# Block sums of weights loaded behind the unit loads, operand sums formed a product sooner, eight PSUM banks in turn

## The chip, the cores and the metric

The kernel runs on one core of a Trainium2 chip. The metric is the device time of one execution in microseconds; several executions are timed and their median is given. The profile is of one such execution. Engines are named as the profile names them: PE (TensorE matmul) and PEld (its weight load), DVE (VectorE), ACT (ScalarE), POOL (GpSimd) and SP, whose queue issues nearly all DMAs.

## The reference

Attention with normalized queries and keys, a feed-forward layer with a squared ReLU, and a gated layer with two more products:

```python
# q, k, v: (4, 12, 448, 64); x: (1792, 768)
q_n, k_n = rmsnorm(q, g_q), rmsnorm(k, g_k)
attn = softmax(q_n @ k_n^T / sqrt(64))
x = rows(attn @ v)                       # (1792, 768)
h = x @ w_in                             # (768, 2048)
x = maximum(h, 0)**2 @ w_out             # (2048, 768)
out = ((x @ w1) * (x @ w2)) @ w3 @ w_out2   # (768, 1024) twice, (1024, 1024), (1024, 768)
```

The weights arrive as 64-bit floats, the rest as 32-bit floats.

## The kernel before

The program walks over 48 attention heads (4 batches of 12) and fills the gaps of each head's chain with matmuls of other work. Beside the heads of batch 0 stands the product of `w3` with the last weight, kept in DRAM as `w3o`; beside those of batch 1 the feed-forward part of batch 0; beside those of batches 2 and 3 first the feed-forward part of batch 1 and then the first product (`w_in`) of batch 2, in `gen_in(PB)`, late in the heads of batch 3. When the heads end, near 945 us, there follows the **tail**, `gen_pair`: `gen_in(PB + 1)`, which is `w_in` for batch 3, and then the products with `w_out` (called L2 here), with `w1` and `w2` (L3) and with `w3o` (L4) for batches 2 and 3 together. L2, L3 and L4 are done as block products by a scheme with seven products instead of eight for a 2 by 2 block matrix. `ORDER2` and `ORDER3` name the seven; `a11`, `a12`, `a21`, `a22` are the operand's blocks, `sums_of` makes the operand sums that products 6, 7 and 4 need, and product 3 needs `a12` less a sum.

Every multiplication is of numbers in two halves: `hi` is the number rounded by an ACT copy to the matmul's type (L112), `lo` the rest, subtracted on POOL or DVE (L120), and three matmuls (L362, L363, L364, in `mm3`) make one product. L120 and L112 are helpers, so the profile's lines for them mix many uses; the tile names tell them apart: `hl` is a weight unit's two halves, `op` an operand's, `quad` the blocks of a weight sum.

Weights come in **units** of 128 by 384 or 128 by 512. `advance` loads a unit into `raw` (L280, six buffers), splits it into `hl` and keeps a few units ahead of the matmul that uses it. Products 5, 4, 7 and 6 need sums of weight blocks. There are 17 of these **sums** (`quads`): six for L2, eight for L3, three for L4. `fetch_next` loads two tiles of 128 by 2 by 512 (or 384) into `quad` (L244), of which four buffers exist, `sum_next` does four subtractions on them and stores two tiles `qs` to DRAM (L260), and the unit loads read them from there. `sum_step` does one `sum_next` for what has been fetched and one `fetch_next`. In `gen_in` it is called for every second product, on POOL (`"g"`) for batch 2 and on DVE (`"v"`) for batch 3.

Instructions of one engine run in the order in which the scheduler of the language put them at build time; it orders by priority and by its own idea of when inputs are there, and a buffer that is free early lets a load move far ahead of the code around it. SP's queue too is in order: a DMA whose wait is not met holds all behind it. The order of the work below is therefore told by the built program, not by the source alone.

In the heads of batches 1 to 3 the softmax result `p` is sent through a DMA to `pw` (L882), and PE transposes `pw` (L903) for the product with `v`.

In L2 a product has eight operand steps `i`, each with three output tiles of three matmuls (nine matmuls), and `form` makes the operand halves `op` some steps ahead by `form2`. `gather` adds a finished product from its PSUM bank to the running sums on DVE (L512). `bank` gives L2's output banks; L3 and L4 take theirs from `ps_mm`, which has three. `after2` turns L2's results into L3's operands.

## Time and profile before

| what | value |
|---|---|
| median of the runs (lowest, highest) | 1292.01 us (1289.71, 1300.1) |
| the profiled execution's own time | 1294.27 us |
| its span in the profile | 1292.5 us |
| PE busy | 1173.5 us (91%), 6078 matmuls |
| PEld, DVE, ACT, POOL busy | 1046.5, 922.3, 737.0, 809.5 us |
| mean granted clock of TensorE | 0.951 |
| 16 DMA engines, mean over the span | 182 GB/s |

The span is what the profiler saw of the program's instructions; 1.8 us of the execution lie outside it. A granted clock of 1.00 is TensorE's upper level of 2.4 GHz and 0.5 its lower of 1.2 GHz; a stretch between the two has some of both. PE at 91% is not PE at its full pace: a matmul at the lower level counts as busy for longer.

### The profile page before, as it was taken

To read this page: it belongs to the slowest core of one execution; us is meant where nothing else is said; L and a number is where in the kernel's file an instruction comes from. 1 tells how busy PE (TensorE), PEld (TensorE's weight loads), DVE (VectorE), ACT (ScalarE), POOL (GpSimd) and SP (SyncE) were. 2 spreads that over 40 slices of the span, in tenths; PEclk is the share of its full clock that TensorE was granted. 3 is DMA by queue.
4 is the path that set the end of the run, shared out by engine and by line. 5 is a ranking of instruction groups with operands and counts; after the bars stand their busy time and mean duration, and the time that the engine had idled before them with its cause. 6 is when DMAs were issued, how large, how long until landed. Compare 5 with 4: busy or idle time off the path is not lost.

```text
span 1292.5 us, 19021 instructions
## 1 busy us (share of the span) xinstructions
PE 1173.5 (91%) x6078; PEld 1046.5 (81%) x6078; DVE 922.3 (71%) x1461; ACT 737.0 (57%) x1595; POOL 809.5 (63%) x772
## 2 busy tenths in 40 slices
PE   7799999988989896589989999999999979899998
PEld 4688888877878786578778888898999969789888
DVE  5798889779978872587889777766432586764574
ACT  5799876667556643455555566656644436433442
POOL 5875536656766677754466565544465779765675
PEclk9799999999989898799999999999999979899999
DMA  7775558888788778677775455554334323233332
GB/s 219 234 239 164 179 176 253 266 292 259 255 237 247 248 248 282 208 230 237 251 256 191 136 151 149 158 162 139 113 102 125 98 65 107 64 109 109 114 125 81
DMA packets 125093, 235.17 MB, mean 182 GB/s; under 512 B 13024, under 2 KB 74688, under 8 KB 124992
## 3 DMA queue, kind: packets, MB, share of 16 engines
q1 hardware_dynamic: 121536, 228.44, 57.2%
q10 hardware_dynamic: 3456, 5.51, 1.2%
q8 instruction: 48, 0.79, 0.3%
q14 instruction: 53, 0.43, 0.1%
HBM read 161.74 MB, written 43.25 MB: 159 GB/s over the span
## 4 chain that ended last, share of the span: by engine, by line
PE 37%; DVE 11%; DMA 6%; POOL 4%; issue 3%; ACT 2%; SPq 0%; POOLq 0%; DVEq 0%; ACTq 0%
PE mm L362 10%; PE mm L363 10%; PE mm L364 10%; DMA pw<-p 2%; DMA quad<-f 2%; PE pt L903 2%; POOL hl L120 1%; ACT p L876 1%; DVE quad L120 1%; POOL quad L120 1%; DVE op L120 1%; PE kv L955 1%; DVE g L120 1%; DVE nb L859 1%; DMA kn<-k_nat 1%
## 5 line engine op out<-in xcount | busy, mean ns | idle before, releaser
L120 POOL TENSOR_TENSOR hl<-raw,hl 128x384 fp32r<-128x384 f32 (+1 forms) x366 | 436.8, 1201 | 221.1 <-ACT hl L112 213.3
L112 ACT ACTIVATE hl<-raw 128x384 fp32r<-128x384 f32 (+1 forms) x399 | 221.3, 563 | 148.2 <-PE mm L364 86.1
L363 PE MATMUL mm<-x,hl 128*128 128x448 f32 (+1 forms) x640 | 239.6, 374 | 9.4 <-POOL x L120 9.4
L362 PE MATMUL mm<-x,hl 128*128 128x448 f32 (+1 forms) x640 | 244.1, 381 | 4.2 <-DVE xf L969 2.0
L364 PE MATMUL mm<-x,hl 128*128 128x448 f32 (+1 forms) x640 | 237.8, 372 | 0.0
L876 ACT ACTIVATE p<-sc,nb,rr 112x448 f32<-112x448 f32 x192 | 137.3, 720 | 121.4 <-DVE nb L860 121.1
L362 PE MATMUL mm<-op,hl 128*128 128x448 f32 x348 | 131.2, 379 | 12.2 <-ACT op L112 8.1
L363 PEld LDWEIGHTS mm<-x,hl 128*128 128x128 f32 x640 | 124.8, 195 | 20.3 <-POOL x L120 11.1
L363 PE MATMUL mm<-act,hl 128*128 128x448 f32 (+1 forms) x352 | 132.7, 377 | 6.8 <-POOL act L120 6.6
L363 PE MATMUL mm<-op,hl 128*128 128x448 f32 x348 | 131.8, 379 | 6.0 <-POOL op L120 5.0
L362 PEld LDWEIGHTS mm<-x,hl 128*128 128x128 f32 x640 | 124.3, 194 | 15.4 <-issue 2.3
L362 PE MATMUL mm<-act,hl 128*128 128x448 f32 (+1 forms) x352 | 134.8, 383 | 0.0
L120 DVE TENSOR_TENSOR ptr<-pt,ptr 128x448 fp32r<-128x448 f32 x144 | 86.5, 617 | 65.3 <-ACT ptr L112 64.8
L364 PEld LDWEIGHTS mm<-x,hl 128*128 128x128 f32 x640 | 124.6, 195 | 10.2 <-POOL hl L120 0.5
L364 PE MATMUL mm<-op,hl 128*128 128x448 f32 x348 | 130.9, 376 | 0.0
L364 PE MATMUL mm<-act,hl 128*128 128x448 f32 (+1 forms) x352 | 130.7, 372 | 0.0
L297 POOL TENSOR_SCALAR raw<-raw 128x384 uint32<-128x384 uint16 (+1 forms) x110 | 80.6, 733 | 74.8 <-DMA raw<-w_in 19.0
L859 DVE TENSOR_REDUCE nb<-sc 112x1 f32<-112x448 f32 x192 | 113.8, 615 | 14.1 <-PE sc L858 12.7
L304 DVE SCALAR_TENSOR_TENSOR raw<-raw 128x384 uint32<-128x384 uint32 (+1 forms) x120 | 88.9, 746 | 37.6 <-POOL hl L120 24.4
L291 ACT ACTIVATE raw<-raw 128x384 f32<-128x384 f32 (+1 forms) x120 | 70.0, 596 | 59.0 <-DMA raw<-w 19.5
L857 PE MATMUL sc<-kt,qh 128*112 128x448 f32 x192 | 76.7, 400 | 26.1 <-ACT p L876 25.1
L903 PE MATMUL pt<-ident_r,pw 112*128 112x112 f32 (+1 forms) x576 | 62.9, 247 | 37.6 <-DMA pw<-p 32.1
(147 smaller groups left out, 2429.3 us busy)
## 6 DMA issues: line engine op xcount, KB each, us to landing
pw<-p SPq DMA_DIRECT2D x72, 392.0 KB, 4.0
raw<-f_in SPq DMA_DIRECT2D x96, 192.0 KB, 2.4
raw<-w_in SPq DMA_DIRECT2D x32, 384.0 KB, 4.9
raw<-w_out SPq DMA_DIRECT2D x24, 512.0 KB, 5.6
raw<-w SPq DMA_DIRECT2D x32, 384.0 KB, 4.2
qt<-q_t SPq DMA_DIRECT2D x48, 224.0 KB, 3.4
raw<-f_out SPq DMA_DIRECT2D x42, 256.0 KB, 2.8
raw<-f SPq DMA_DIRECT2D x56, 192.0 KB, 2.4
```

The lines of the kernel that those rows point to most:

```text
L112: nc.scalar.activation(out=out, in_=in_, func=AF.Copy)
L120: e.tensor_tensor(out=out, in0=in0, in1=in1, op=ALU.subtract)
L291: nc.scalar.activation(out=hi, in_=hi, func=AF.Prelu, scale=2.0**-112, alpha=-(2.0**32))
L297: nc.gpsimd.tensor_scalar(out=t[:, :n, 0], in0=low, scalar1=2.0**-13, scalar2=2.0**-14 - 0.5, op0=ALU.mult, op1=ALU.add)
L304: nc.vector.scalar_tensor_tensor(out=f[:, :n].bitcast(U32), in0=t[:, :n, 1], scalar=3, in1=t[:, :n, 0], op0=ALU.logical_shift_left, op1=AL ...
L362: nc.tensor.matmul(ps, w[:, 0, wk, :], x[0], start=(i == 0), stop=False)
L363: nc.tensor.matmul(ps, w[:, 0, wk, :], x[1], start=False, stop=False)
L364: nc.tensor.matmul(ps, w[:, 1, wk, :], x[0], start=False, stop=(i == last))
L857: nc.tensor.matmul(o[j], d["qh"][:, c * P:(c + 1) * P], d["kt"], start=True, stop=False)
L859: nc.vector.tensor_reduce(out=nb[:, j:j + 1], in_=o[j], axis=AX.X, op=ALU.max, negate=True)
L876: nc.scalar.activation(out=p, in_=o[j], func=AF.Exp, scale=d["rq"][:, c:c + 1], bias=nb[:, j:j + 1], accum_out=sm[:, i, c:c + 1],)
L903: nc.tensor.transpose(to[:kn, c * P:(c + 1) * P], d["p"][c][:, k0:k0 + kn], one)
```

## The change

Five edits. (1) In `fetch_next` each load of a `quad` may not stand ahead of the last unit load that the source has issued (`issue_after`). (2) `gen_in` calls `sum_step` three times for each batch (products 2, 7 and 12) instead of eight, the loop that finished all sums ahead of L2 goes, and `sum_step("v")` is called behind each of L2's seven products and after each group of seven in L3. (3) `sums_of` and the subtraction for product 3 run one product sooner, behind product 2's and product 6's operands; the spare tiles of L2 take other buffers for that. (4) `form` runs four steps ahead in L2 instead of three. (5) The output tiles of L2, L3 and L4 go round eight banks of four pools.

```diff
     def fetch_next():
...
-            nc.sync.dma_start(out=t, in_=src)
+            with tc.issue_after(last["load"]):
+                nc.sync.dma_start(out=t, in_=src)
...
     def load_next():
...
-            nc.sync.dma_start(out=t[:, :n], in_=src)
+            last["load"] = nc.sync.dma_start(out=t[:, :n], in_=src).ins
...
     def gen_in(b):
...
-            if m % 2:
+            if m % 5 == 2:
                 sum_step("g" if b == PB else "v")
...
-    def bank(k):
-        if k % 2 == 0:
-            return ps_mm.tile([128, 512], F32, name="mm", tag="mm")[:, :S]
+    banks = [(ps_mm, "mm"), (ps_sc, "sc"), (ps_mm, "mm"), (ps_pt, "pt")]
+    banks += [(ps_mm, "mm"), (ps_sc, "sc"), (ps_kv, "kv"), (ps_pt, "pt")]
+
+    def bank():
+        pool, tag = banks[turn["ps"] % len(banks)]
         turn["ps"] += 1
-        pool, tag = ((ps_sc, "sc"), (ps_sc, "sc"), (ps_pt, "pt"))[turn["ps"] % 3]
         return pool.tile([128, 512], F32, name=tag, tag=tag)[:, :S]
...
     def gen_pair():
         yield from gen_in(PB + 1)
-        while pos["sum"] < len(quads):
-            sum_step("v")
...
         def form2(k, i):
+            src = {1: a[i][0], 2: a[i][1], 6: a[i][0], 7: spare.get(i), 4: a[i][3], 5: a[i][2], 3: a[i][1]}[k]
+            t = parts(src, xp, "x", "v" if i % 2 else "g")
+            if k == 2:
+                if i < 4:
+                    spare[i] = t2.tile([128, S], F32, name="s3", tag=("khl", "vhl")[i // 2])
+                elif i % 2 == 0:
+                    x = xp.tile([128, 2, S], F32, name="s3", tag="x")
+                    spare[i], spare[i + 1] = x[:, 0, :], x[:, 1, :]
+                sums_of(a[i], spare[i])
             if k == 6:
...
-                sums_of(a[i], spare[i])
-            if k == 3:
                 sub_on("v", a[i][1], a[i][1], a[i][0])
...
-            ps = [bank(m) for _ in range(NQ)]
+            ps = [bank() for _ in range(NQ)]
...
-                    form(m * n + at + 3, form2)
+                    form(m * n + at + 4, form2)
...
             after2(k)
+            sum_step("v")
```

In L3 `ps` comes from `bank()` and `sum_step("v")` stands behind each group of seven products; in L4 `ps` comes from `bank()` too and `form4` moves its sums as `form2` does.

What moves where, from the built programs. The number behind a name counts buffers; before and after count differently from L2 on.

**SP's queue, in the heads of batch 2.** `f_in` and `f_out` units are of the feed-forward part of batch 1. Before:

```order
L260 DMA qs3_0_116<-quad_10255 128x1024
L260 DMA qs3_1_117<-quad_10257 128x1024
L280 DMA raw_5905<-f_in_106 128x384
L260 DMA qs4_0_118<-quad_10373 128x1024
L746 DMA qt_5889<-q_t 128x448
L882 DMA pw_5829<-p_5826 112x896
L280 DMA raw_5938<-f_in_106 128x384
```

After:

```order
L282 DMA raw_5905<-f_in_106 128x384
L752 DMA qt_5889<-q_t 128x448
L282 DMA raw_5938<-f_in_106 128x384
L888 DMA pw_5829<-p_5826 112x896
L282 DMA raw_5957<-f_in_106 128x384
```

Loads and stores of the sums are gone from here. In the changed program the first load of a `quad` stands in `gen_in(PB)`, behind a unit of `f_in` for batch 2.

**SP's queue and DVE, where L2's product 4 ends and product 5 runs.** `f_out_107` and `f_1_108` are units of products 3 and L3's first; `qs10` and `quad_12226` are sums 10 and 11 of the 17. SP, before:

```order
L280 DMA raw_12113<-f_out_107 128x512
L280 DMA raw_12118<-f_out_107 128x512
L280 DMA raw_12171<-f_out_107 128x512
L280 DMA raw_12176<-f_out_107 128x512
L280 DMA raw_12181<-f_1_108 128x384
```

SP, after:

```order
L262 DMA qs10_1_131<-quad_12050 256x1x384
L282 DMA raw_12065<-f_out_107 128x512
L282 DMA raw_12118<-f_out_107 128x512
L282 DMA raw_12123<-f_out_107 128x512
L262 DMA qs10_0_130<-quad_12048 256x1x384
L282 DMA raw_12128<-f_1_108 128x384
L246 DMA quad_12226<-f_2_109 128x2x384
L246 DMA quad_12228<-f_2_109 128x2x384
```

DVE in the same place, after (`op_12157` is an operand of product 3, the rows of L514 gather product 5):

```order
L120 TENSOR_TENSOR op_12157<-g_10296,op_12157 128x448
L120 TENSOR_TENSOR quad_12048<-quad_12048,quad_12050 128x384
L120 TENSOR_TENSOR quad_12226<-quad_12228,quad_12226 128x384
L120 TENSOR_TENSOR quad_12228<-quad_12228 128x384
L120 TENSOR_TENSOR quad_12228<-quad_12228,quad_12226 128x384
L514 TENSOR_TENSOR c_12021<-pt_12052,u_11876 128x448
L514 TENSOR_TENSOR u_11731<-pt_12052,u_11731 128x448
```

Four subtractions of the sums stand between an operand of product 3 and the gather of product 5, and a store of sum 10 stands ahead of the load of sum 11 on SP; before, DVE went from the one to the other with nothing between.

**DVE, in `gen_in(PB + 1)`.** The rows of L505 or L507 make the `g` tiles of batch 3. Before:

```order
L505 TENSOR_TENSOR g_10802<-mm_10756,r_10800 128x448
L505 TENSOR_TENSOR g_10802<-mm_10757,r_10818 128x448
L505 TENSOR_TENSOR g_10862<-mm_10831,r_10860 128x448
L505 TENSOR_TENSOR g_10862<-mm_10864,r_10893 128x448
L505 TENSOR_TENSOR g_10937<-mm_10906,r_10935 128x448
```

After:

```order
L507 TENSOR_TENSOR g_10752<-mm_10706,r_10750 128x448
L120 TENSOR_TENSOR s3_11361<-g_9787,g_10752 128x448
L507 TENSOR_TENSOR g_10752<-mm_10707,r_10768 128x448
L120 TENSOR_TENSOR s3_11377<-g_9787,g_10752 128x448
L120 TENSOR_TENSOR quad_10810<-quad_10812,quad_10810 128x512
```

Of the 24 instructions of `sums_of` in L2, 12 (those of steps 0 to 3) now stand on DVE ahead of the last `g` tile, and with them sums 3, 4 and 5 of the weights; before, all 24 stood behind the last `g` tile, between operands of product 2 and of product 7.

## Rows read from the trace of the kernel before

**Rows 1.** Busy time by stretch, matmuls of L362 alone: window, length, engines (xcount), PEclk, DMA.

```profile
510.40:683.80 173.40, 58.46 (x144) 30.13 (x144) 0.90 0.75 239
700.90:751.90 51.00, 19.82 (x53) 9.83 (x53) 1.00 0.48 140
751.90:850.00 98.10, 40.38 (x108) 20.18 (x108) 1.00 0.53 157
```

**Rows 2.** What touches `quad`: ns min/median/max, first and last start; DMA landing.

```profile
L120 DVE TENSOR_TENSOR quad<-quad x40: 543/560/1667, 552.1 to 688.7; 128x384 f32<-128x384 f32 x28, 128x512 f32<-128x512 f32 x12
L120 POOL TENSOR_TENSOR quad<-quad x28: 994/1290/1795, 435.5 to 531.1; 128x512 f32<-128x512 f32 x24, 128x384 f32<-128x384 f32 x4
L260 SPq DMA_DIRECT2D qs<-quad x34: 319/531/977, 445.1 to 693.8; - x34
DMA to landing us min/median/max: 2.6/4.4/7.0
```

**Rows 3.** Waits of PE, 420 to 700 us: total us, times, longest.

```profile
PE pt L903 <- DMA pw<-p: 28.2, 7, 13.5
PE sc L857 <- ACT p L876: 14.1, 7, 3.1
```

**Rows 4.** SP's queue in order of time: start us, us, line, DMA.

```profile
505.42 0.32 SPq L260 DMA_DIRECT2D qs<-quad  x1
...
506.31 0.74 SPq L882 DMA_DIRECT2D pw<-p  x1
...
533.06 1.27 SPq L280 DMA_DIRECT2D raw<-f_in  x2
...
536.47 0.54 SPq L882 DMA_DIRECT2D pw<-p  x1
```

**Rows 5.** ACT and PE in order of time, same stretch.

```profile
492.53 0.71 ACT L876 ACTIVATE p<-sc,nb,rr 112x448 f32<-112x448 f32 x1
...
510.56 0.99 PE L903 MATMUL pt<-ident_r,pw 112*128 112x112 f32 x6 [9.85 <-DMA pw<-p]
...
542.03 0.99 PE L903 MATMUL pt<-ident_r,pw 112*128 112x112 f32 x6 [13.50 <-DMA pw<-p]
```

**Rows 6.** Busy time of all engines by stretch of the tail.

```profile
1030.00:1060.00 30.00, 23.18 (x81) 19.55 (x80) 28.33 (x34) 10.94 (x21) 19.48 (x14) 0.77 0.21 68
1060.00:1100.00 40.00, 40.00 (x200) 37.05 (x199) 26.43 (x26) 22.40 (x42) 39.31 (x28) 1.00 0.32 99
1100.00:1122.00 22.00, 15.80 (x64) 13.60 (x63) 18.08 (x21) 10.78 (x21) 18.27 (x14) 0.77 0.18 55
1122.00:1138.00 16.00, 14.73 (x73) 13.32 (x72) 11.71 (x14) 6.69 (x14) 12.02 (x11) 1.00 0.31 90
...
1226.00:1242.00 16.00, 12.12 (x49) 10.39 (x50) 16.00 (x23) 5.47 (x11) 10.60 (x8) 0.89 0.32 99
```

**Rows 7.** Waits of PE, 950 us to the end.

```profile
PE mm L362 <- ACT op L112: 8.1, 3, 4.8
PE mm L363 <- POOL op L120: 5.0, 4, 1.8
PE mm L362 <- DVE u L512: 4.1, 2, 2.8
```

**Rows 8.** Groups by form on POOL and DVE: 945 to 1005, then 1060 to 1100.

```profile
L120 POOL TENSOR_TENSOR hl<-raw,hl 128x512 fp32r<-128x512 f32 x6 | 7.7, 1294 | 2.5 <-ACT hl L112 2.4
...
L120 POOL TENSOR_TENSOR x<-xf,x 128x448 fp32r<-128x448 f32 x1 | 1.2, 1156 | 0.1
...
L120 POOL TENSOR_TENSOR hl<-raw,hl 128x512 fp32r<-128x512 f32 x16 | 24.2, 1535 | 0.0
...
L120 DVE TENSOR_TENSOR op<-g,op 128x448 fp32r<-128x448 f32 x9 | 12.4, 1388 | 10.5 <-ACT op L112 10.5
```

**Rows 9.** PE in order of time near 1112 us.

```profile
1112.25 1.49 PE L362 MATMUL mm<-op,hl 128*128 128x448 f32 x3 [4.82 <-ACT op L112]
1115.12 0.74 PE L363 MATMUL mm<-op,hl 128*128 128x448 f32 x1 [1.38 <-POOL op L120]
```

More of the change, by code (lines that the diff above doesn't have):

```diff
@@ L231, in attention_moe_kernel @@
     fetched = {}
+    last = {}
     def is64(i):
@@ L573, in form2 @@
         def form2(k, i):
-            if k == 6:
-                if i % 2 == 0:
-                    t = xp.tile([128, 2, S], F32, name="s3", tag="x")
-                    spare[i], spare[i + 1] = t[:, 0, :], t[:, 1, :]
-                sums_of(a[i], spare[i])
-            if k == 3:
+            src = {1: a[i][0], 2: a[i][1], 6: a[i][0], 7: spare.get(i), 4: a[i][3], 5: a[i][2], 3: a[i][1]}[k]
[7 more added lines that the diff above has]
+                sums_of(a[i], spare[i])
+            if k == 6:
                 sub_on("v", a[i][1], a[i][1], a[i][0])
-            src = {1: a[i][0], 2: a[i][1], 6: a[i][0], 7: spare.get(i), 4: a[i][3], 5: a[i][2], 3: a[i][1]}[k]
-            return parts(src, xp, "x", "v" if i % 2 else "g")
+            return t
         todo = [(k, i) for k in ORDER2 for i in range(n)]
@@ L665, in gen_pair @@
                 for k in ORDER3:
-                    ps = ps_mm.tile([128, 512], F32, name="mm", tag="mm")[:, :S]
+                    ps = bank()
                     ww = use(u)
@@ L675, in gen_pair @@
                             nc.vector.tensor_tensor(out=got[i], in0=got[i], in1=av[i], op=ALU.mult)
+                sum_step("v")
         n = NIC // 2
@@ L682, in form4 @@
             a11, a12, a21, a22 = ab[i]
-            if k == 6:
-                if i % 2 == 0:
-                    t = xp.tile([128, 2, S], F32, name="s3", tag="x")
-                    spare4[i], spare4[i + 1] = t[:, 0, :], t[:, 1, :]
-                sums_of(ab[i], spare4[i])
-            if k == 3:
-                sub_on("v", a12, a12, a11)
             src = {1: a11, 2: a12, 6: a11, 7: spare4.get(i), 4: a22, 5: a21, 3: a12}[k]
             pool, tag = ((t2, "kn"), (t2, "kn"), (t3, "ptr"), (t3, "ptr"))[i] if k == 1 else (actp, "act")
-            return parts(src, pool, tag, "v" if i % 2 else "g")
+            t = parts(src, pool, tag, "v" if i % 2 else "g")
+            if k == 2:
+                if i % 2 == 0:
+                    x = xp.tile([128, 2, S], F32, name="s3", tag="x")
+                    spare4[i], spare4[i + 1] = x[:, 0, :], x[:, 1, :]
+                sums_of(ab[i], spare4[i])
+            if k == 6:
+                sub_on("v", a12, a12, a11)
+            return t
         todo = [(k, i) for k in ORDER2 for i in range(n)]
@@ L698, in gen_pair @@
             for e in range(NQ):
-                ps = ps_mm.tile([128, 512], F32, name="mm", tag="mm")[:, :S]
+                ps = bank()
                 ww = use(u)
```

## The prediction

> **What bounds the kernel now.** I read the strip of forty slices first, since a program with several stages has several limits. PE is busy for 7 to 9 tenths nearly everywhere and its clock strip dips in two regions: 420 to 700 us and 1030 to 1240 us. Between them, from 700 to 1030, PE is nearly full at a granted clock of 1.00. So the time is PE's own work plus what these two regions lose, and each has its own cause.
>
> In the first region I compared paces. L362 is one third of the feed-forward matmuls and its count tells how far the fill has come, whatever the clock. It moves on by 144 in 173.4 us, 1.204 us for each, where the heads of batch 2 run with the feed-forward part of batch 1; right behind, with the same mixture of heads and fill, it takes 51.0/53 = 0.962 us, and then 98.1/108 = 0.908 [rows 1]. (Some matmul records can be missing, which hits all three alike.) The 17 weight sums lie exactly in the slow stretch and just ahead of it: 28 subtractions on POOL from 435.5 to 531.1, 40 on DVE from 552.1 to 688.7, and 34 stores on SP [rows 2].
>
> How they cost time is seen best around 500 us. The waits of PE there are for `pw`: 28.2 us in 7 waits, the longest 13.5, and 14.1 us for `p` [rows 3]. ACT had both halves of `p` by 493.2, but SP issued the `pw` DMA only at 506.31, directly behind a store of a sum at 505.42 and a load of `qt` [rows 4, 5]; PE then waited 9.85 us. The same again at 542.03, after 13.50 us: `pw` was issued at 536.47, behind unit loads at 533.06 that waited for buffers which POOL, busy with sums, had not freed [rows 4, 5]. The queue is in order, so a store that waits for a subtraction holds a transfer that PE needs at once.
>
> In the tail, PE's full pace is 200 matmuls in 40 us, 0.2 us each [rows 6]. Against that I count the loss of four stretches as length less 0.2 us for each matmul: A, 1030 to 1060, 30 - 81 x 0.2 = 13.8; B, 1100 to 1122, 22 - 64 x 0.2 = 9.2; C, 1122 to 1138, 16 - 73 x 0.2 = 1.4; D, 1226 to 1242, 16 - 49 x 0.2 = 6.2. In A, DVE is busy 28.33 of 30 us, in D 16.00 of 16 [rows 6]: the operand sums. The waits fit: 8.1 us for operands from ACT, 5.0 for operands from POOL, and 4.1 for `u` on DVE, which is a gather that has not freed its bank [rows 7]. The rest of the loss is matmuls at a lower clock behind each wait: 0.77 granted in A and B, between the two levels [rows 6].
>
> **The change part by part.** *Middle.* No sum is left there. The heads of this window should run at the pace that the next heads show: 144 x (1.204 - 0.962) = 34.8 us gained; at the faster pace of 0.908 it would be 42.6; as a floor I take only the waits for `pw` other than the first, 28.2 - 9.85 = 18.4 [rows 1, 3]. The first wait lies ahead of that window and ends with it: 9.85 us [rows 5] and a few matmuls at the lower clock, 10, between 0 (if something else holds `pw`) and 12. I take 44.8 together.
>
> *Tail, gains.* A: half of `sums_of` moves under `gen_in(PB + 1)`, and the rest a whole product ahead, so DVE's block of work no longer stands just ahead of product 6's and 7's operands. I take 12 of the 13.8, at worst 6. C and the gather part of D are banks: eight in turn instead of three let a gather be late by several products of L3, so C goes (1.4), and of D's 6.2 I take 5 (2 to 6.2), since the last operand of L4's first product still comes from L3's last products. B is another matter. It stands where L2's product 3 needs operands while DVE and ACT are filled with product 5's gather and L3's operands [rows 9]. `form` a step earlier frees the third operand, but the fourth stands behind the same queue; and DVE now has four subtractions of weight sums between product 3's operand and the gather, of which three need a load that SP issues behind the store of sum 10. That load takes 4.4 us, at most 7.0 [rows 2]. I put B at 1 us worse, between 7 better and 4 worse.
>
> *Tail, costs.* The 17 sums do not vanish. Two run on POOL under the last heads: 8 subtractions of 1.29 us, 10.3 us of POOL [rows 2], where POOL is about half idle; I take 2, between 0 and 10. One follows there on DVE and three under `gen_in(PB + 1)`, where the strip shows DVE at 2 tenths: nothing, and 2.2 us for each (four of 0.56) if that cover were gone. By DVE's order six fall in L2 and five in L3. In L3 DVE has about half its time and operands are long made: nothing. In L2 the matter is that DVE and POOL slow each other: the `hl` subtraction of POOL takes 1.294 us beside `gen_in` and 1.535 in L2, and DVE's operand subtraction 1.388, where a sum's takes 0.543 at least [rows 2, 8]. In 1060 to 1100, POOL does 28 instructions beside 26 of DVE [rows 6], so each of DVE's lengthens POOL's by about 28 x 0.241/26 = 0.26 us. L2 gets 24 subtractions more and loses the 12 of `sums_of` that went ahead: 12 x 0.26 = 3.1 us of POOL, which has 0.7 of 40 us to spare there [rows 6]. I take 3, between 0 and the 13.4 that 24 x 0.56 us would make with nothing overlapped. Loads of sums that land late hold DVE's queue for a moment before three of the gathers: 1 us, between 0 and 7.
>
> By what rows 8 show, the two engines' instructions stretch but still overlap: alone, 16 `hl` of 1.294 and 12 more of 1.156 are 34.6 us of POOL, and 17 DVE instructions with both inputs in SBUF (26 less nine gathers) at 0.54 are 9.2, together 43.8, done in 40 us. The Trainium skill (SBUF — State Buffer, SBUF: two separate sides) calls the port pair that DVE and GpSimd share an exclusive lock, in which the later instruction blocks until the other is done. The rows agree that they hinder each other, not that nothing overlaps; by the rule as it stands L2 would have no room for the sums, which is the second rival.
>
> *Sum.* 1292.5 - 34.8 - 10 - 12 - 1.4 - 5 + 1 + 2 + 3 + 1 = 1236.3 for the span. The profiled execution had 1.8 us outside its span and was 2.3 us above the median of the runs, so I predict 1236.3 + 1.8 - 2.3 = 1235.8, rounded to **1236**.
>
> **The rivals.** *First: the middle is paced by the softmax chain.* The waits of PE for `p`, 14.1 us, and a DVE that is busy there for 6 to 8 tenths without the sums too, speak for it; the quicker heads behind, with the same chain, speak against. Then only the waits for `pw` go, 18.4 + 10 instead of 44.8: 1236 + 16.4 = 1252. *Second: DVE and POOL take turns.* The 24 subtractions in L2 go onto PE's path in full, 13.4 instead of 3: 1236 + 10.4 = 1246. Speaking against it: 43.8 us of work in 40. *Third: the queue holds in the tail as it did in the middle.* On SP the stores of a sum now stand between unit loads of L2 and L3, and a store waits for DVE. If each of the 15 sums behind the first two costs what the sums cost now, 44.8/17 = 2.6 us, 39.5 us come back (4 of it already counted): 1236 + 35.5 = 1271. *Fourth, on the other side: that hold becomes a starved PE in L2.* L2 has six sums and its units are used every 2.4 us (twelve matmuls of 0.2). If each store held the loads as long as in the middle, (9.85 + 13.50)/2 = 11.7 us, it would cost 70 us against a gain of 56: 1236 + 70 - 4 = 1302. It decides against the change from 56/6 = 9.4 us for each sum on. Against it stands that in the middle the held DMA was `pw`, which PE needs at once, while a unit is loaded about seven units, 17 us of L2, before its use. That the sums stay where they were, so that the change does nothing in the middle, is excluded by SP's rows.
>
> **How the numbers follow.** Chances: forecast 0.57, first rival 0.15, second 0.12, third 0.08, fourth 0.05, and 0.03 for more than forecast (the pace of 0.908 and B gone too, 1236 - 7.8 - 8 = 1220 and below). One per cent, about 13 us, is what a measurement here can tell from no change, so faster means under 1279: the forecast and the first two rivals wholly, most of the third: 0.90. Within one per cent 0.05, slower 0.05. The range reaches from 1214 (all gains near their upper ends) to 1264, past the first two rivals with the other costs at their upper halves; left out are the third and fourth and the ends.
>
> **What would show it.** In the profile after: no `quad` ahead of the last heads; waits of PE for `pw` between 420 and 700 below 8 us; L362 at 0.91 to 0.98 us in the heads of batch 2; the 15 later sums on DVE, most at 0.55 to 1.6 us; A with under 3 us of loss, no wait for a gather in L3 or at the start of L4, but still a wait of 5 us or more in B for an operand. The sum is wrong if the heads of batch 2 keep a pace of 1.1 or more, or if PE waits in L2 for weights (`hl`).

## The result and the profile after

The changed kernel took 1279.32 us (median of 5 runs, 1272.78 to 1282.69) beside 1292.72 us for the kernel before on the same chip (5 runs): a ratio of 0.988, with a 95% interval of 0.9837 to 0.9923. The forecast was 1236, with a range from 1214 to 1264. The direction held; a quarter of the gain came. The profiled execution took 1276.58 us, its span is 1274.8.

To see where the time went I cut both spans at the same points of the work: at the additions `xf<-kv,vt` of the heads (48 of them, numbered from 0), at the first matmul that reads `op`, and at the 505th and the 1009th such matmul (504, 504 and 252 of them are L2, L3 and L4). Lengths in us, from the start times in the trace:

| stretch | before | after | difference |
|---|---|---|---|
| heads 0 to 14 | 262.9 | 260.8 | -2.1 |
| heads 14 to 36, the middle | 506.7 | 459.7 | -47.0 |
| heads 36 to 42 | 97.6 | 99.1 | +1.5 |
| heads 42 to 47, the last heads | 77.6 | 90.5 | +12.9 |
| to the first operand matmul | 57.2 | 57.1 | -0.1 |
| L2 | 125.6 | 139.6 | +14.0 |
| L3 | 108.4 | 102.3 | -6.1 |
| L4 and the end | 56.5 | 65.7 | +9.2 |

The middle gave what was forecast, and the rest of the program gave most of it back. First the middle. Busy time by stretch, matmuls of L364 alone (L362 before), answering to [rows 1]: window, length, engines (xcount), PEclk, DMA share, GB/s.

```profile
490.56:637.57 147.01, 54.56 (x145) 27.59 (x145) 0.98 0.51 145
...
654.20:802.21 148.01, 59.89 (x160) 30.18 (x161) 1.00 0.51 150
```

Waits of PE of the changed kernel, 420 to 700 us, answering to [rows 3].

```profile
PE pt L909 <- DMA pw<-p: 10.2, 8, 3.3
PE sc L863 <- ACT p L882: 9.1, 4, 3.5
```

The windows are cut so that the same matmuls stand in them as in the windows of [rows 1]: 147.01 us where 173.4 were. That is 1.02 us for each of 144, not yet the 0.962 that I took as the pace without sums. The waits for `pw` fell from 28.2 to 10.2 us, and the longest from 13.5 to 3.3. What this window fell short of, the stretch ahead of it made good: the 87 matmuls of L362 from 420 us on took 90.40 us, and the same ones now run from 422.83 to 490.56, 67.73 us.

Next, what touches `quad` in the changed kernel, answering to [rows 2]: ns min/median/max, first and last start; then what DVE waited for.

```profile
L120 DVE TENSOR_TENSOR quad<-quad x60: 543/1044/1642, 890.7 to 1171.0; 128x384 f32<-128x384 f32 x32, 128x512 f32<-128x512 f32 x28
L262 SPq DMA_DIRECT2D qs<-quad x34: 319/439/1245, 829.2 to 1172.5; - x34
...
L120 POOL TENSOR_TENSOR quad<-quad x8: 1289/1299/1361, 825.1 to 862.7; 128x512 f32<-128x512 f32 x8
...
  DMA quad<-f: 16.5, 3
  DMA quad<-f_out: 11.1, 5
  DMA quad<-w3o: 10.2, 3
```

Of the 68 subtractions 12 now run under the last heads, 12 between them and L2, 24 in L2 and 20 in L3. The median on DVE is 1044 ns; in the middle it was 560. The two engines stood still 37.8 us for loads of the blocks to be summed, DVE for 31.1 of it.

The last heads and the tail by stretch, answering to [rows 6]: window, length, PE, PEld, DVE, ACT, POOL busy (xcount), PEclk, DMA share, GB/s. The four are the last heads, L2, L3 and L4; then L2 of the kernel before.

```profile
819.60:910.12 90.52, 82.24 (x438) 73.90 (x437) 56.15 (x91) 50.15 (x114) 47.08 (x44) 0.94 0.56 175
967.18:1106.78 139.60, 114.74 (x506) 102.13 (x504) 103.83 (x108) 57.79 (x109) 101.52 (x72) 0.89 0.46 149
1106.78:1209.12 102.34, 102.34 (x505) 94.58 (x504) 81.31 (x103) 39.01 (x77) 74.24 (x63) 1.00 0.61 196
1209.12:1274.78 65.66, 55.10 (x253) 49.11 (x251) 34.60 (x50) 23.01 (x41) 40.18 (x28) 0.92 0.29 95
```

```profile
1001.98:1127.61 125.63, 112.61 (x506) 101.17 (x504) 89.09 (x96) 58.06 (x109) 100.85 (x72) 0.90 0.27 84
```

L3 is full: PE is busy for all of its 102.34 us at a granted clock of 1.00, although five sums run there and the DMA share is at 0.61. L2 and L4 are not. Waits of PE in the tail, 950 us to the end, answering to [rows 7].

```profile
PE mm L364 <- ACT op L112: 9.2, 1, 9.2
PE sc L364 <- ACT op L112: 7.0, 1, 7.0
PE pt L365 <- DVE op L120: 6.2, 2, 5.1
PE kv L365 <- DVE op L120: 2.8, 1, 2.8
PE mm L365 <- DVE op L120: 2.4, 1, 2.4
PE mm L366 <- POOL hl L120: 2.1, 2, 1.8
```

No wait for a gather (`u` on DVE) is left, but a wait of 9.2 us and one of 7.0 us for a single operand are new. The longest before was 4.8. How the first arises is seen in order of time: SP, DVE, ACT and PE where product 5 of L2 has ended and product 3 runs, the place that [rows 9] show. The first line is the last matmul of product 5.

```profile
1071.53 0.37 PE L366 MATMUL sc<-op,hl 128*128 128x448 f32 x1
...
1072.84 1.61 DVE L120 TENSOR_TENSOR quad<-quad 128x384 f32<-128x384 f32 x1
...
1074.48 0.53 SPq L262 DMA_DIRECT2D qs<-quad  x1
...
1075.71 1.10 SPq L246 DMA_DIRECT2D quad<-f  x2
...
1081.62 1.75 DVE L120 TENSOR_TENSOR quad<-quad 128x384 f32<-128x384 f32 x3 [7.17 <-DMA quad<-f]
1083.28 0.62 DVE L514 TENSOR_TENSOR c<-pt,u 128x448 f32<-128x448 f32 x1
...
1083.93 0.58 ACT L112 ACTIVATE op<-c 128x448 fp32r<-128x448 f32 x1 [11.55 <-DVE c L514]
...
1091.22 1.03 ACT L112 ACTIVATE op<-g 128x448 fp32r<-128x448 f32 x2
...
1091.83 0.74 PE L364 MATMUL mm<-op,hl 128*128 128x448 f32 x1 [9.24 <-ACT op L112]
```

Read it from the bottom. PE waits for the fourth operand of product 3 (`op<-g`). ACT made it late because it does its work in order too: ahead of this operand it had operands of L3 to make (`op<-c`), and for the first of them it had waited 11.55 us for a gather. That gather, of product 5, was free to run after 1071.9 but stood behind subtractions of weight sums in DVE's queue: the fourth of one sum (1.61 us) and three of the next (1.75 us), of which the first waited 7.17 us for its load. SP had issued that load only at 1075.71, behind a store of the sum before at 1074.48, which had waited for that sum's fourth subtraction at 1072.84. Nothing in this stretch of PE's work waits for a finished sum.

The wait at the start of L4, in order of time: DVE, ACT and PE.

```profile
1210.94 1.68 DVE L679 TENSOR_TENSOR ab<-ab,a 128x448 f32<-128x448 f32 x1
1212.54 1.68 DVE L120 TENSOR_TENSOR ab<-ab 128x448 f32<-128x448 f32 x1
...
1217.45 0.58 ACT L112 ACTIVATE op<-ab 128x448 fp32r<-128x448 f32 x1 [7.44 <-DVE ab L679]
...
1218.08 0.74 PE L364 MATMUL sc<-op,hl 128*128 128x448 f32 x1 [6.97 <-ACT op L112]
```

DVE is busy without a break there: operand sums of L4 (`ab<-ab`, L120) stand among the last gathers and multiplications of L3, and one of them takes 1.68 us. That was so before as well. The kernel before, DVE in order of time at the end of L3:

```profile
1225.06 3.17 DVE L120 TENSOR_TENSOR ab<-ab 128x448 f32<-128x448 f32 x2
...
1238.99 0.61 DVE L675 TENSOR_TENSOR ab<-ab,a 128x448 f32<-128x448 f32 x1
```

In both kernels 13 of the 16 instructions that make L4's operand sums stand on DVE ahead of the last multiplication of L3 (the second line here).

### The profile page after: what moved, and what is told of

Same layout as the page of the kernel before. It is cut to its first block, busy times and chain, and to the rows that moved or that the text cites. A ratio compares the mean times of both kernels' runs of the same rounds, so it can differ in the third digit from the quotient of the medians.

```text
span 1274.8 us, 19031 instructions
## 1 busy us (share of the span) xinstructions
PE 1164.1 (91%) x6078; PEld 1038.9 (81%) x6078; DVE 951.3 (75%) x1481; ACT 737.8 (58%) x1595; POOL 792.4 (62%) x752
## 4 chain that ended last, share of the span: by engine, by line
PE 39%; DVE 10%; DMA 9%; POOL 6%; issue 5%; ACT 4%; SPq 0%; POOLq 0%; ACTq 0%; DVEq 0%
PE mm L364 9%; PE mm L365 8%; PE mm L366 8%; DMA pw<-p 4%; POOL hl L120 4%; PE pt L909 2%; ACT p L882 2%; PE kv L961 1%; DMA quad<-f 1%; PE sc L364 1%; PE sc L365 1%; PE sc L366 1%; DMA raw<-w 1%; DVE nb L865 1%; PE pt L365 1%
## 5 line engine op out<-in xcount | busy, mean ns | idle before, releaser
L120 POOL TENSOR_TENSOR hl<-raw,hl 128x384 fp32r<-128x384 f32 (+1 forms) x366 | 443.2, 1221 | 224.2 <-ACT hl L112 213.0
L364 PE MATMUL mm<-x,hl 128*128 128x448 f32 (+1 forms) x640 | 242.0, 378 | 2.8 <-DVE gf L437 1.3
L365 PEld LDWEIGHTS mm<-x,hl 128*128 128x128 f32 x640 | 123.1, 192 | 19.6 <-POOL x L120 10.8
L365 PE MATMUL mm<-act,hl 128*128 128x448 f32 (+1 forms) x352 | 130.8, 372 | 6.2 <-POOL act L120 4.3
L120 DVE TENSOR_TENSOR ptr<-pt,ptr 128x448 fp32r<-128x448 f32 x144 | 86.3, 617 | 65.8 <-ACT ptr L112 65.4
L364 PEld LDWEIGHTS mm<-x,hl 128*128 128x128 f32 x640 | 123.1, 192 | 13.3 <-DVE gf L437 1.7
L364 PE MATMUL mm<-act,hl 128*128 128x448 f32 (+1 forms) x352 | 132.2, 375 | 0.9 <-ACT act L436 0.5
L366 PEld LDWEIGHTS mm<-x,hl 128*128 128x128 f32 x640 | 122.9, 192 | 10.3 <-POOL hl L120 0.8
L366 PE MATMUL mm<-act,hl 128*128 128x448 f32 (+1 forms) x352 | 129.3, 368 | 0.0
L293 ACT ACTIVATE raw<-raw 128x384 f32<-128x384 f32 (+1 forms) x120 | 70.2, 598 | 56.6 <-DMA raw<-w 26.1
L120 DVE TENSOR_TENSOR quad<-quad 128x384 f32<-128x384 f32 (+1 forms) x60 | 64.5, 1075 | 38.9 <-DMA quad<-f 16.5
L909 PEld LDWEIGHTS pt<-ident_r,pw 112*128 112x128 f32 (+1 forms) x576 | 53.2, 135 | 32.8 <-DMA pw<-p 23.0
L112 ACT ACTIVATE ptr<-pt 128x448 fp32r<-128x448 f32 x144 | 74.0, 543 | 9.4 <-PE pt L909 9.1
```

The costliest lines, as they stand in the source:

```text
L112: nc.scalar.activation(out=out, in_=in_, func=AF.Copy)
L120: e.tensor_tensor(out=out, in0=in0, in1=in1, op=ALU.subtract)
L293: nc.scalar.activation(out=hi, in_=hi, func=AF.Prelu, scale=2.0**-112, alpha=-(2.0**32))
L364: nc.tensor.matmul(ps, w[:, 0, wk, :], x[0], start=(i == 0), stop=False)
L365: nc.tensor.matmul(ps, w[:, 0, wk, :], x[1], start=False, stop=False)
L366: nc.tensor.matmul(ps, w[:, 1, wk, :], x[0], start=False, stop=(i == last))
```

## The experiments

Every kernel was timed against the kernel before on its own chip (medians there 1296.99, 1298.55 and 1297.04 us for the three groups, e1 to e4, e5 to e8, e9 to e12). The ratio has its 95% interval in brackets. The stretches of all of them, cut as above, in us, each from its one profiled execution:

| kernel | median | ratio | 14 to 36 | 36 to 42 | 42 to 47 | to L2 | L2 | L3 | L4 |
|---|---|---|---|---|---|---|---|---|---|
| before | | | 506.7 | 97.6 | 77.6 | 57.2 | 125.6 | 108.4 | 56.5 |
| after | 1279.32 | 0.988 [0.9837, 0.9923] | 459.7 | 99.1 | 90.5 | 57.1 | 139.6 | 102.3 | 65.7 |
| e1 tail edits alone | 1290.34 | 0.995 [0.9934, 0.9966] | 507.4 | 97.8 | 77.2 | 57.2 | 116.7 | 102.1 | 65.5 |
| e2 sums moved alone | 1289.5 | 0.9937 [0.9913, 0.996] | 463.0 | 98.6 | 91.1 | 57.2 | 144.7 | 114.8 | 56.6 |
| e3 no sums | 1246.35 | 0.9622 [0.9592, 0.9651] | 463.4 | 98.0 | 78.8 | 57.2 | 117.6 | 104.2 | 63.3 |
| e4 queued behind, not moved | 1294.94 | 0.9986 [0.9973, 1.0] | 463.3 | 98.7 | 106.4 | 57.5 | 139.1 | 110.8 | 56.7 |
| e5 no stores | 1269.69 | 0.978 [0.9749, 0.981] | 462.4 | 97.8 | 89.4 | 57.2 | 131.9 | 102.1 | 64.8 |
| e6 no subtractions | 1249.9 | 0.9619 [0.9588, 0.9649] | 462.1 | 97.9 | 84.7 | 57.2 | 118.5 | 104.2 | 63.8 |
| e7 subtractions alone | 1269.26 | 0.9771 [0.9746, 0.9797] | 489.8 | 97.6 | 78.1 | 57.2 | 117.4 | 104.2 | 63.2 |
| e8 behind the gather | 1264.95 | 0.9736 [0.9701, 0.977] | 463.1 | 97.9 | 88.5 | 57.2 | 125.2 | 102.1 | 63.4 |
| e9 and none under heads | 1261.43 | 0.9726 [0.9709, 0.9743] | 462.9 | 98.6 | 78.6 | 61.3 | 127.5 | 102.1 | 65.2 |
| e10 L4's sums late | 1273.88 | 0.9817 [0.9795, 0.9839] | 461.3 | 98.3 | 87.9 | 57.2 | 138.8 | 102.7 | 61.2 |
| e11 subtractions in place | 1256.44 | 0.9687 [0.9672, 0.9701] | 463.2 | 99.4 | 83.2 | 57.2 | 123.0 | 102.1 | 64.8 |
| e12 all three | 1257.04 | 0.9695 [0.9679, 0.9711] | 461.8 | 97.9 | 78.3 | 61.2 | 128.4 | 104.2 | 59.4 |

The question was where some 40 us of the forecast gain went. My theory: the moved sums cost in the tail much more than the 6 us that I gave them. Rival: the tail's own edits (operands sooner, eight banks) did not bring the 18.4 us. Within the theory two mechanisms compete: the time of the subtractions on DVE and POOL, or the hold that a queue in order puts on work behind an instruction that waits.

**e1, e2 and e4: the parts alone.** e1 is the changed kernel with the sums as they were before; against the changed kernel:

```diff
-            if m % 5 == 2:
+            if m % 2:
...
         yield from gen_in(PB + 1)
+        while pos["sum"] < len(quads):
+            sum_step("v")
...
             after2(k)
-            sum_step("v")
```

The step in L3 and the queueing of the loads are gone as well.

> The sums stay where the kernel before has them; only the operand sums a product sooner, form four steps ahead and eight banks are taken over. If the tail's new loss comes from the weight sums (late loads or shared time), these three edits alone still win most of A, C and D of the prediction: 1274 to 1280 us. If the three edits themselves win nothing (the waits for a bank only turn into waits for an operand): 1288 to 1296 us.

e2 is the kernel before with the same lines the other way about: the sums moved, the tail as it was.

```diff
-            if m % 2:
+            if m % 5 == 2:
...
             after2(k)
+            sum_step("v")
```

> The sums are moved as in the changed kernel (loads behind unit loads, the new places of the steps), the rest is as before. The middle wins its 45 to 50 us as in the changed kernel. If the weight sums cost the tail and the three other edits win, this is worse than the changed kernel by what they win, 1290 to 1300 us. If the three edits win nothing, it is as the changed kernel, 1276 to 1283 us.

e4 is the kernel before with only the queueing of the loads:

```diff
+            with tc.issue_after(last["load"]):
-            nc.sync.dma_start(out=t, in_=src)
+                nc.sync.dma_start(out=t, in_=src)
```

> The kernel before with one edit: the loads of the sums stay behind the unit loads. The 17 sums then fall under the last heads (POOL) and the product with w_in for batch 3 (DVE), none in L2 to L4. If the sums hurt in L2 to L4 because DVE is busy there: the middle's 45 to 50 us less some 10 to 20 for eight sums on POOL under the heads, 1255 to 1268 us. If the sums cost the same wherever they stand, 2.6 us each: 1285 to 1295 us.

The two halves add up: 0.995 x 0.9937 = 0.9887, where both together gave 0.988. So in total neither hides the other, and both fell short. By stretch they do not add up: L3 is 6.3 us shorter in e1 and 6.4 longer in e2, yet 6.1 shorter with both, while L2 is 14.0 longer with both where 10.1 would be the sum. e1 shows the tail's edits alone: L2 8.9 us shorter, L3 6.3 shorter, L4 9.0 longer, 6.2 in all of 18.4. Waits of PE in e1, 950 us to the end; the first stands at the start of L4, the others in L2.

```profile
PE sc L363 <- ACT op L112: 7.0, 1, 7.0
PE pt L364 <- DVE op L120: 4.2, 1, 4.2
PE mm L363 <- ACT op L112: 3.0, 1, 3.0
```

The 7.0 us at the start of L4 are there without a sum near it. e4 shows that the queueing does the moving: without the steps of the new places, the sums already leave the middle (463.3 us) and crowd into the last heads and the stretch up to 1005 us. There they cost 28.8 us under the last heads and 13.5 in L2, and the kernel is as fast as before: moving the sums to this place alone gains nothing.

**e3: no sums at all.** The units of products 5, 4, 7 and 6 read plain blocks in place of the sums, so this kernel computes other products; all else is the changed kernel.

```diff
-        sum_of[len(units)] = n
-        return {5: sx[:, 0, :], 4: sx[:, 1, :], 7: sy[:, 0, :], 6: sy[:, 1, :]}[k]
+        return {5: x[:, 0, :], 4: x[:, 1, :], 7: y[:, 0, :], 6: y[:, 1, :]}[k]
...
     def sum_step(eng):
+        return
```

> The changed kernel with the weight sums left out wholly: no loads, subtractions or stores of sums; products 5, 4, 7 and 6 read plain blocks of the weights in the same number and size, so the output is another. If the sums cost the tail and the last heads 25 to 31 us: 1245 to 1255 us, with B no longer than 8 us. If the loss in the tail is of the operand sums and banks: 1268 to 1278 us.

0.9622 against 0.988: the sums still cost about 33 us where they are now, 11.7 under the last heads, 22.0 in L2, -1.9 in L3 and 2.4 in L4. In the middle they save nothing more (463.4 against 459.7), so that window is now free of them. L2 of e3, columns as above:

```profile
959.00:1076.61 117.61, 107.57 (x506) 97.10 (x504) 83.17 (x84) 59.09 (x109) 100.59 (x72) 0.96 0.31 89
```

Beside the changed kernel's 139.60 us, 14.8 of the 22.0 are waits of PE and 7.2 are matmuls that took longer (114.74 us busy in place of 107.57), at a granted clock of 0.89 in place of 0.96. L3 and L4 together differ by only 0.5 us.

**e5 to e7: stores, DMAs or subtractions.** In all three the units read what e3 reads or unsubtracted blocks, so the products are others. e5 loads and subtracts but does not store:

```diff
-        for dst, t in zip(sums[n], (x, y), strict=True):
-            nc.sync.dma_start(out=dst, in_=t)
```

> The changed kernel with the sums loaded and subtracted but not stored; products 5, 4, 7 and 6 read plain blocks, so the output is another. Theory 1 (hold): on SP the store of one sum, which waits for DVE, holds the load of the next, that lands late, and DVE's queue waits for it with a gather behind. Without stores the loads are early: 1252 to 1264 us. Theory 2 (time): the subtractions cost by their own time and by sharing with POOL: 1270 to 1282 us, hardly changed.

e6 loads and stores but does not subtract:

```diff
-        sub_on(eng, x[:, 0, :], y[:, 0, :], x[:, 0, :])
-        sub_on(eng, y[:, 0, :], y[:, 1, :], y[:, 0, :])
-        sub_on(eng, y[:, 1, :], y[:, 1, :], x[:, 0, :])
-        sub_on(eng, x[:, 1, :], x[:, 1, :], y[:, 1, :])
```

> The changed kernel with the sums loaded and stored unsubtracted, so the output is another; DVE and POOL do nothing for them. Theories 1 and 2 both expect 1246 to 1258 us, near the kernel without any sums. If it is the traffic and the queue of SP by themselves that cost (unit loads late): 1268 to 1282 us.

e7 moves no data of the sums and makes each subtraction on a tile of zeros:

```diff
+        z = zero[:, :x.shape[-1]]
+        for t in (x[:, 0, :], y[:, 0, :], y[:, 1, :], x[:, 1, :]):
+            sub_on(eng, t, z, z)
```

> The changed kernel with all 68 subtractions in their places, but on a tile of zeros, with no loads and stores of sums; products 5, 4, 7 and 6 read plain blocks, so the output is another. Theory 1 (hold): nothing waits for a load, 1248 to 1258 us. Theory 2 (time): 1268 to 1282 us.

e6 moves all the data of the sums and is as fast as no sums at all (0.9619 and 0.9622). L2 of e6, columns as above:

```profile
964.86:1083.32 118.46, 108.86 (x506) 99.14 (x504) 83.12 (x84) 58.95 (x109) 99.84 (x72) 0.93 0.54 180
```

180 GB/s, more than in the changed kernel, and 0.9 us longer than without. In L2 the transfers cost next to nothing by themselves. Under the last heads this execution lost 5.9 us; it is the slowest of e6's four (1253.06 us, the median is 1249.9), and by the ratios e6 is no slower than e3, so these 5.9 are not shown to be of the transfers.

e5 takes 7.7 us off L2, so a third of its loss hangs on the stores; the load at 1075.71 above shows one way, being issued behind a store. But the loads of e5 are late too: DVE still waited 16.5 us for them in L2. Waits of SP's queue in L2 (us in total, times, longest), first of e5, then of the changed kernel; then one of e5's loads in order of time, POOL and SP.

```profile
SPq L279 <- POOL hl L120: 107.0, 41, 12.8
```

```profile
SPq L282 <- POOL hl L120: 30.8, 21, 5.7
SPq L262 <- DVE quad L120: 28.8, 5, 11.9
```

```profile
1092.62 1.32 POOL L120 TENSOR_TENSOR hl<-raw,hl 128x384 fp32r<-128x384 f32 x1
...
1093.97 0.32 SPq L279 DMA_DIRECT2D raw<-f  x1
1094.38 0.39 SPq L245 DMA_DIRECT2D quad<-f  x1
```

By edit (1) a load of a sum stands behind a unit load, and the unit load waits for a `raw` buffer, which POOL frees when it has made the `lo` of an earlier unit. All seven pairs of loads in L2 of e5 were issued 0.4 us behind a unit load, and that within 0.1 us of the end of such a subtraction on POOL. So the change itself makes these loads late, with or without the stores. Of the five loads that DVE waited for in L2 of the changed kernel, three were let go by a store ahead of them on SP and two by such a unit load.

e7 did not do what I meant: with no load to wait for, the 68 subtractions ran in the middle.

```profile
L122 DVE TENSOR_TENSOR quad<-zero x60: 536/677/4557, 438.7 to 509.2; 128x384 f32<-128x384 f32 x32, 128x512 f32<-128x512 f32 x28
```

There, with no DMA of a sum, they cost 489.8 - 463.4 = 26.4 us, where the sums of the kernel before cost 506.7 - 463.4 = 43.3. So subtractions can cost the heads much without any hold on SP's queue. It does not split the 43.3: here 60 of them were crowded onto DVE within 71 us, and in the kernel before 28 ran on POOL and 40 on DVE over 253 us.

**e11: the subtractions in their places.** As e7, with each subtraction behind the last subtraction or addition that its engine had been given (or the last `g` tile).

```diff
+            with tc.issue_after(last[eng]):
-            sub_on(eng, t, z, z)
+                sub_on(eng, t, z, z)
```

> Subtractions alone as in the run before it (on zeros, no loads and stores of sums, plain blocks read, another output), but each behind the last instruction that its engine was given, so that they stay in the tail. This is the price of their own time and of sharing with POOL, with nothing to wait for: if that is small, 1248 to 1256 us; if time is most of the tail's loss, 1266 to 1280 us.

Now they run from 854.3 to 1153.6 us, in the last heads and the tail. Busy time of L2 in e11, columns as above; then groups by form in L2 of e11 (busy us, mean ns | idle before), the subtractions and the weight halves on POOL; last, that POOL group in L2 of e3, without sums.

```profile
963.41:1086.44 123.03, 110.15 (x506) 98.48 (x504) 113.17 (x107) 59.14 (x109) 104.52 (x72) 0.93 0.30 86
```

```profile
L123 POOL TENSOR_TENSOR hl<-raw,hl 128x512 fp32r<-128x512 f32 x38 | 59.2, 1585 | 4.3 <-ACT hl L115 3.5 <-POOL op L123 0.8
...
L123 DVE TENSOR_TENSOR quad<-zero 128x384 f32<-128x384 f32 x20 | 26.8, 1397 | 0.0
```

```profile
L120 POOL TENSOR_TENSOR hl<-raw,hl 128x512 fp32r<-128x512 f32 x38 | 56.6, 1516 | 5.1 <-ACT hl L112 3.9 <-issue 1.1
```

L2 is 5.4 us longer than with no sums, and the last heads, with the eight subtractions of POOL alone, 4.4. That is the price of the work itself, and it is small against 22.0 and 11.7.

**e8, e9, e10 and e12: other orders, whole sums.** These compute all that the kernel before computes. e8 puts the subtractions of a sum behind the last addition that its engine was given, which is the end of the product's gather or, behind product 5, the last addition of `after2`:

```diff
+        with tc.issue_after(last[eng]) if eng in last else ExitStack():
-        sub_on(eng, x[:, 0, :], y[:, 0, :], x[:, 0, :])
+            sub_on(eng, x[:, 0, :], y[:, 0, :], x[:, 0, :])
...
```

> The changed kernel with the subtractions of a sum ordered on DVE behind the last addition that the source has issued (the product's gather), so that a late load holds no gather in L2 and L3. Theory 1 (hold), with the gather as what is held: 1260 to 1270 us. Theory 2 (time): 1276 to 1284 us, unchanged.

e9 adds to it that no sum runs under the last heads and six steps under `gen_in(PB + 1)`:

```diff
-            if m % 5 == 2:
-                sum_step("g" if b == PB else "v")
+            if b > PB and m % 3 == 0:
+                sum_step("v")
```

> As e8, and the three steps of the sums in the first product of batch 2 are given up for six in that of batch 3 (products 0, 3, 6, 9, 12, 15), so that no sum falls under the last heads. If the sums on POOL and SP's hold of pw cost the last heads their 10 to 12 us: 1250 to 1258 us, and no loss in the product with w_in for batch 3. If those heads are slower for another reason, or the six sums crowd the other stage: 1262 to 1268 us, as e8.

e10 is the changed kernel with L4's operand sums behind L3's last multiplication:

```diff
+                with tc.issue_after(last["mul"]):
-                sums_of(ab[i], spare4[i])
+                    sums_of(ab[i], spare4[i])
```

> The changed kernel with L4's operand sums ordered on DVE behind the last multiplication of L3. If L4's first product waits (7 us) because DVE does those sums ahead of L3's last gathers and multiplications: the wait shrinks to under 3 us and the time is 4 to 8 us less than the changed kernel, 1272 to 1278 us. If the wait is the plain length of the chain from L3's last product to the operand: no change, 1278 to 1284 us.

e12 is e9 with the edit of e10.

> The changed kernel with subtractions behind the gather, no sums under the heads and L4's operand sums late, all at once. If each of the three removes its own wait: 1244 to 1254 us. If they only move work into one another: 1258 to 1266 us.

e8 is the experiment that decides for L2. It does the same work with the same DMAs; what differs is DVE's order, and with it when SP's stores are free to go (the four subtractions of one sum slid from L2 into L3). Busy time of L2, then DVE in order of time at the place that was shown above of the changed kernel:

```profile
967.97:1093.12 125.15, 109.69 (x505) 98.92 (x504) 108.43 (x104) 59.26 (x109) 103.04 (x72) 0.92 0.48 159
```

```profile
1065.61 0.60 DVE L515 TENSOR_TENSOR u<-pt,u 128x448 f32<-128x448 f32 x1
...
1076.87 1.54 DVE L515 TENSOR_TENSOR c<-c 128x448 f32<-128x448 f32 x1
1078.33 0.55 DVE L120 TENSOR_TENSOR quad<-quad 128x384 f32<-128x384 f32 x1
```

The gather runs first, the subtractions fill DVE's free time behind it, and L2 takes 125.2 us in place of 139.6. In L2 no wait of DVE for a load of a sum is left; in the changed kernel there were five, 22.8 us together (two of them, 6.2 us, the profile calls "issue"; each ends 0.1 us behind the landing of a load). Of the 14.4 us, 5.6 fall in product 6 (21.4 to 15.8 us) and 4.9 in product 3 (35.0 to 30.1). In product 6 of the changed kernel the form is the same as above, with two gathers behind the wait:

```profile
1009.89 0.56 DVE L120 TENSOR_TENSOR quad<-quad 128x384 f32<-128x384 f32 x1 [5.76 <-DMA quad<-f]
1010.37 0.61 DVE L514 TENSOR_TENSOR c<-mm,u 128x448 f32<-128x448 f32 x1
```

In product 3, the place shown above, most of the wait is left: PE's two waits for operands go from 11.6 to 10.0 us together, and without any sums (e3) they are 5.8.

e9 removes the cost under the last heads, 88.5 to 78.6 us, and pays part of it back behind them: 4.1 us up to L2, 2.3 in L2 and 1.8 in L3 and L4. Against e8 its total differs by less than the intervals. e10 takes away the 7.0 us at the start of L4; the longest wait of PE in L4 is then 2.6.

```profile
1208.76:1269.98 61.22, 53.87 (x253) 48.15 (x251) 42.14 (x52) 22.03 (x41) 38.31 (x28) 0.97 0.30 100
```

L4 went from 65.7 to 61.2, not back to 56.5. But the end of L3 and the start of L4 trade with each other: L3 and L4 together take 164.9 us before, 167.7 in e1, 168.0 in the changed kernel and 163.9 in e10. e12, all three, is the fastest kernel that does the whole work: 1257.04 us, 0.9695, which beats the kernel before and the changed one.

Not all fell where they were expected. e2 (1289.5), e9 (1261.43) and e11 (1256.44) missed a range by under 1 us, e5 (1269.69) and e12 (1257.04) lie between their two ranges, near the second: stores are not the whole of the hold, and e12's three edits in part move work into one another. e1, e4 and e7 fell in the second of their ranges, e7 with the subtractions in another place than meant; e3, e6, e8 and e10 in the first.

## Why the prediction was off, point by point

**The middle came out as forecast, its division by luck.** 44.8 us were forecast between the heads of batch 2 and the wait ahead of them; 47.0 came, and 43.3 in e3, where this part has no sums either. Two errors cancelled: the measured window gave 26.4 us in place of 34.8, since its pace went to 1.02 and not to 0.962 us, and the stretch ahead of it gave 22.7 in place of 10. Both belong to sums that leave this part. How they cost time there is shown only in part: PE's waits for `pw` fell by 18.0 us and those for `p` by 5.0, and the granted clock of the window rose from 0.90 to 0.98. I had put it down to `pw` behind a store on SP; e7 shows that subtractions without any DMA can cost these heads 26.4 us, and no run splits the 43.3.

**The step that failed is the tail's costs.** I gave the seventeen sums in their new places 2 + 3 + 1 = 6 us in all. e3 shows what they cost there: about 34 us by stretches, 33 by the medians. Three terms stand in it, and the first is the largest.

- *The load that lands late*, "holds DVE's queue for a moment before three of the gathers: 1 us, between 0 and 7". It is 14.4 us in L2 (139.6 to 125.2, e8 against the changed kernel). I counted how long a load takes, 4.4 us, but not that the subtractions wait for it in order, ahead of gathers whose operands PE needs next, nor how late the load is issued: behind a store that waits for DVE, or behind a unit load that waits for POOL. That hold was in the text for SP and `pw` in [rows 4, 5]; I did not look for the same form on DVE. Leaving out the stores takes off 7.7 us (e5). e8 takes the wait and the subtractions' own time away from the gathers at once; how the 14.4 divide between the two is not shown. At the one place shown above they are 7.17 and 3.4 us of DVE.
- *Two sums under the last heads*, taken at 2 us between 0 and 10, and a third there on DVE, taken at nothing: 11.7 us (90.5 against 78.8 in e3), all of it gone in e9. POOL's eight subtractions alone cost 4.4 (e11), and PE's waits for `pw` there are 6.4 us where e3 has 2.2; the rest is not divided. A price was at hand, my own 2.6 us for a sum in the middle, 7.8 for three; e4, with more of them under these heads, lost 28.8. I had taken POOL's idle time there as cover.
- *The sharing of DVE and POOL in L2*, taken at 3 us between 0 and 13.4: 5.4 us with the subtractions alone (e11), 7.5 with their loads and stores and the order of e8, 7.2 of these in product 3. The size was about half of that, and the second rival, all in full at 13.4, is out. Beside 21 more subtractions, POOL's 38 `hl` of one form went from 56.6 to 59.2 us; all its 72 instructions in L2 took 104.52 us where e3's took 100.59, 0.19 us for each subtraction where I had 0.26 from [rows 6, 8], so 3.9 us together; DVE is the one that stretches, 1397 ns in place of 543. The Trainium skill (SBUF — State Buffer, SBUF: two separate sides) calls the shared port pair of the two engines an exclusive lock, held for a whole instruction. As an estimate by that rule, the 21 subtractions at 0.543 us each would add up to 11.4 us on POOL if POOL were held by every one of them; the trace has 3.9.

**The tail's gains were the second miss.** A, C and D were to give 12 + 1.4 + 5 = 18.4 us, less 1 for B; e1 alone gave 6.2. A and B lie in L2, which gained 8.9 in e1: 7.9 in products 2 and 6, where 12 were forecast for A (a wait of 4.2 us is left there), and 0.9 in product 3, where B still is two waits of 3.0. C and D were to give 6.4 at the end of L2 and in L3 and L4; L3 became full and 6.3 us shorter, L4 9.0 longer, 2.8 lost together. The step is "of D's 6.2 I take 5". I had read that DVE is busy for 16.00 of 16 us in D with operand sums, and yet bought the time with banks. Eight banks let PE run past the gathers, and then it stood 7.0 us for the first operand of L4, since DVE had the same work in the same order to do, L4's operand sums among L3's last gathers. e10, which only moves these sums behind them, takes that wait away and 4.4 us of L4.

**The rivals.** The first, a middle paced by the softmax chain, is out: 47.0 us came. The third, the queue holds in the tail as in the middle, gave 1271 and came nearest (1279.32); its price for a sum was 2.6 us, and 33/17 = 1.9 came. That is in part luck, for its place was another: it had unit loads on SP held behind stores, whereas the hold that matters in L2 is DVE's, ahead of a gather. The fourth, a PE starved of weights, is not seen: the waits for `hl` in the tail are 4.2 us together. I gave it and the third 13 in 100 between them, and that was where the chance was misplaced: the change took a hold away from one queue, and the first question was on which queue it would stand next.

**The signs.** As forecast came the late place of the sums, the 15 later ones on DVE at 0.54 to 1.64 us, no wait for a gather, and a wait of 5 us or more in B (9.2). Missed were the waits for `pw` (10.2 us, not below 8), the pace in the heads of batch 2 (1.02, not 0.91 to 0.98) and A, where a wait of 5.1 us stands alone against a loss of under 3.

**What stays open.** How the 14.4 us divide between late loads and the subtractions' own time in front of gathers: no run put the loads ahead of the unit loads in L2, or left the subtractions where they are with loads on time. Why L3 and L4 together gain only 1.0 us in e10 (164.9 to 163.9) where 6.4 were forecast for C and D. And what in the middle cost the 43.3 us, beyond the waits named above.

## What to carry to other kernels

Before moving background work behind the loads of the foreground, write down for each engine that it touches which urgent instruction will stand behind it in that engine's order, and what the background instruction waits for: subtractions that waited for a load in front of a gather cost 14.4 us here, the subtractions by themselves 5.4. Ask of the load too what it will stand behind. Price moved work by what it costs at the place where it lands, with a kernel that leaves it out as the bound, and not by the idle share of the engine there. More buffers turn a wait for a buffer into a wait for the next thing that was made too late, so look up at the same time the order in which that is made.

## What the runs showed of the hardware that I had not expected

DVE's subtraction of two SBUF operands is 543 ns at least and 1397 ns on average in L2 beside a POOL that is busy for 85% of the time (104.52 of 123.03 us, e11), while POOL's `hl` lengthened only from 1516 (e3) to 1585 ns by these 21 subtractions: DVE bears the larger part. Gathers, which read one input from PSUM, stay at 0.61 us in the same stretch. The transfers of the sums, on the other hand, showed next to no price in L2 and L3: 0.9 us in L2 of e6, at 180 GB/s, and in L3 of the changed kernel, with 0.61 of the DMA engines busy, PE was busy without a gap at a granted clock of 1.00.
